# Re-timing the row-halved first layer: attention work ahead at the entry, the reload early in the last tile, three second-layer weights converted during attention

## The chip, the cores and the metric

The kernel runs on one core of one Trainium2 chip. The metric is the device time of one execution in microseconds, the median over repeated runs. Five in-order instruction streams share the work: TensorE (PE, matrix products), VectorE (DVE), ScalarE (ACT), GpSimd (POOL) and SyncE (SP), which issues the DMA transfers. They meet only at semaphores.

## The reference

```
x = attention(q, k, v, i_gate, f_gate, o_gate)   # gated linear attention, 4 x 8 heads, 768 steps, width 40
x = x.transpose(0, 2, 1, 3).reshape(3072, 320)
h = x @ w_in            # first layer, 320 -> 2048
x = relu(h) ** 2 @ w_out   # 2048 -> 320
h = x @ w2_in           # second layer, 320 -> 2048
g = where(h > 0, h, exp(min(h, 0)) - 1)
return g @ w2_out       # 2048 -> 320
```

## The kernel before

Attention is cut into 24 units (u) of chunks; its result, transposed, is the input of the first layer. Both layers work on 6 token tiles j of 512 tokens and on NF = 16 slices m of 128 of the hidden width. A step k stands for one (layer, j, m). Every fp32 operand of a product is held as a high part (rounded for the fast product) and a low part (the difference), so each product is three matmuls.

**First layer.** Tiles j = 0 and 1 use matmuls of all 128 rows (L477 for the first product, L538 for the second). Tiles 2 to 5 use the upper and lower 64 rows of the array as two independent streams ("row halves": L576 first product, L595 second product). They run in `cycle(k, fill)`, one for each four steps (k = 32, 36, ..., 92). A cycle is 62 positions of the two streams; other engines' work is hung on positions by `at(i, f, ...)`, and what stands at a position follows, on its engine, what stands at an earlier one. ACT and DVE apply the relu (L504 on ACT, L502 on DVE), ACT squares (L486), DVE makes the low part `glo` or `gt` (`elem_lo`, L522). `handed` (L561) is a one-element ACT instruction that reads a PSUM bank and so makes the next writer wait for it: its row reads `room`.

The cycles k = 32 to 76 carry attention (`fill_attention`): transposes of the last unit's result (`xt`, L367), value products (L304, L309), `scores` (L292), the DVE multiplication of scores with the mask `mb` (`emit_P`, L299), the normalisation (`norm`, L350 to L353, ending in `xt`), gates (`gate_exp`: `gaw`, L199). Step k = 30 is the entry: it is written out by hand and begins the row-halved form.

**The reload.** The first layer's sums go through `put_bank` (a copy from PSUM: `y`, L602 on ACT, L604 on DVE) to the scratch tensor `y_dr` (L605), and come back for the second layer by `y_load` (`yr`, L827, 768 KB in two DMAs). There is one `yr` buffer. `y_split(j, c)` turns chunk c (of 5) into a high part on ACT (L843) and a low part on DVE (L844).

**Weights.** A weight slice is loaded as packed integers (`raw`, L125), and made into two fp32 parts by `w_top` (`cu`, ACT, L130), `w_low` (`ct`, ACT, L135), `w_add` (DVE, L140), `w_hi` (POOL, L144) and `w_lo` (DVE, L150). The `raw` pool has three buffers; in the cycles with attention two of them are used as `gt`. The 16 slices of the second layer are NF to NF+15. The last tile's cycles (k = 80, 84, 88, 92) carry `fill_last(c)`, c = 0 to 3, which holds the reload of tile 0 and the conversions.

**Second layer.** Pairs of steps: `first_pair(k + 2)` (two first products on the two row halves, L756), then `second_half(k - 2)` and `second_half(k)` (L787). ACT makes `r`, `th`, `ex` (L512 to L514), DVE `ex`, `r` (L515, L516), POOL `ghi` (L517), DVE `glo` (L522). In its tile j = 0 it converts the last slices and splits tile 1's input between the pairs; the later tiles split only.

Of the kernel before, what the change touches and what calls it, by code (L numbers as in the profile page):

```python
# [63 lines left out]
def body(tc, qk, kvo, gates, wq, ident_in, out):  # L64
# [50 lines left out]
    w_n = [0] * 4  # L115

    def w_load(i):
        t = raws[i] = rawp.tile([128, 4 * WC + 32], I16, tag="raw", name="raw")
        l, f = ftiles[i]
        sp.dma_start(out=t[:, 1:1 + 4 * WC], in_=wq[l, f].bitcast(I16))  # L125

    def w_top(i):
        t = tops[i] = cvu.tile([128, WC], F16, tag="cu", name="cu")
        r = raws[i].bitcast(BF16)[:, 4:4 + 4 * WC].rearrange("p (n four) -> p n four", four=4)
        act.activation(out=t, in_=r[:, :, 0], func=AF.Copy)  # L130

    def w_low(i):
        u = low[i] = cvt.tile([128, WC], I32, tag="ct", name="ct")
        r = raws[i].bitcast(U32)[:, 1:1 + 2 * WC].rearrange("p (n two) -> p n two", two=2)
        act.activation(out=u, in_=r[:, :, 0], func=AF.Copy, scale=2.0 ** -13)  # L135

    def w_add(i):
        t = whole[i] = low.pop(i)
        u = t.bitcast(U16).rearrange("p (n two) -> p n two", two=2)[:, :, 1]
        dve.tensor_tensor(out=u, in0=u, in1=tops.pop(i).bitcast(U16), op=ALU.add)  # L140

    def w_hi(i):
        W[ftiles[i]] = wp.tile([128, 2 * WC], F32R, tag="w", name="w")
        pool_.tensor_scalar(out=W[ftiles[i]][:, 0:WC], in0=whole[i].bitcast(F32), scalar1=1.0, scalar2=1.0, op0=ALU.mult, op1=ALU.mult)  # L144

    def w_lo(i):
        l, f = ftiles[i]
        w, t = W[l, f], whole.pop(i)
        for a, k, o in [(640, 64, WC), (0, 640, WC + 64)] if l == 0 else [(0, WC, WC)]:
            dve.tensor_tensor(out=w[:, o:o + k], in0=t[:, a:a + k].bitcast(F32), in1=w[:, a:a + k].bitcast(F32), op=ALU.subtract)  # L150

    def w_next(which, *fs):
        i = w_n[which]
        w_n[which] += 1
        for f in fs:
            f(i)
# [546 lines left out]
    def fill_attention(k):  # L703

        u = (k + 21) // 4
        t = 4 * u + 1
        out = []
        def at(i, f, *a):
            out.append((i, f, *a))
        def products():  # L710
            ps = bank(u, "s")
            if B <= u - 1 < NU:
                for f in trans(u - 1, ps):
                    f()
# [18 lines left out]
        at(36, units, u + 1, scores)  # L733
        at(36, units, u + 1, lambda v: emit_P(2 * v), lambda v: emit_P(2 * v + 1))
        at(38, gate_at, t + 15, gate)
        at(42, gate_at, t + 15, gate_exp)
        at(44, gate_at, t + 15, gate_store)
        at(44, units, u + 1, o_tanh, wk_mult)
        at(45, units, u + 2, lambda v: mask(2 * v), lambda v: mask(2 * v + 1))
        return out  # L740

    def first_pair(k):
# [17 lines left out]
    def second_ops(k, i):  # L760

        l, j, m, _ = steps[k]
        w, cs, ops = W[l, m + 1], slice(i * L, (i + 1) * L), []
        for x in range(2):
            hi, lo, _ = G[k + x]
            wh, wl = (w[:, o + 384 * x:o + 384 * x + DM] for o in (0, WC))
            ops += [(hi[:, cs], wh), (hi[:, cs], wl), (lo[:, cs], wh)]
        return ops

# [60 lines left out]
    def y_split(j, c):  # L830

        t = YR[j]
        if c == 0:
            X[NTILE + j] = []
            for x in range(2):
                if j % 2:
                    a, b_ = (xp.tile([128, n, TT], F32R, tag=tag, name=tag) for n, tag in ((3, "xh"), (3, "xl")))
                    X[NTILE + j].append([a[:, i] for i in range(3)] + [b_[:, i] for i in range(2)])
                else:
                    a = bp["x"].tile([128, 5, TT], F32R, tag=f"x{x}", name=f"x{x}")  # L840
                    X[NTILE + j].append([a[:, i] for i in range(5)])
        hi, lo = (X[NTILE + j][x][c] for x in range(2))
        act.activation(out=hi, in_=t[:, c], func=AF.Copy)  # L843
        dve.tensor_tensor(out=lo, in0=t[:, c], in1=hi.bitcast(F32), op=ALU.subtract)  # L844
        if c == 3:
            dve.tensor_tensor(out=t[:, 4], in0=t[:, 4], in1=t[:, 5], op=ALU.add)

    mp_t = {}
# [122 lines left out]
    }  # L971
    for word in ORDER.split():
        tasks[word[0]](int(word[1:]))
    w_n = [NF] * 4

    nt, nm = NK + 21, NK + 2

    def first(k):
# [6 lines left out]
            nm += 1  # L985
        return todo

    def convert(i):
        w_top(i)
        w_low(i)  # L990
        if i + 3 < 2 * NF:
            w_load(i + 3)
        w_add(i)

    def fill_last(c):

        n = [0, 2, 5, 8, 11][c:c + 2]
        todo = [NF + i for i in range(*n)]
        out = []
        if c == 0:  # L1000
            out += [(0, w_load, NF), (20, w_load, NF + 1), (20, w_load, NF + 2), (20, y_load, 0)]
        if c == 3:
            out += [(0, y_load, 1)]
        if len(todo) > 2:
            i = todo.pop(0)
            out += [(11, convert, i), (12, w_hi, i), (26, w_lo, i)]
        a, b = todo
        out += [(37, convert, a), (45, convert, b), (46, w_hi, a), (57, w_lo, a), (57, w_hi, b), (61, w_lo, b)]
        out += [(i, y_split, 0, x) for i, x in ([(52, 0)], [(18, 1), (52, 2)], [(18, 3), (52, 4)], [])[c]]
        return out  # L1010

    for k in range(NK, len(steps)):
# [15 lines left out]
        if k + 2 == JP * NF:  # L1028
# [7 lines left out]
            attn_mul(t)  # L1036
            for f in mm2(k):
                f()
            zipped(lower, upper)
            elem(k + 2)  # L1040
            elem_lo(k + 2)
            attn_post(t)
            attn_pre(t + 1)
            attn_pe(t + 1)
            for f in mm2(k + 1):
                f()
            elem(k + 3)
            elem_lo(k + 3)
            put(k + 1)
            attn_mul(t + 1)  # L1050
            attn_post(t + 1)
            units((t + 1) // 4, o_tanh, wk_mult)
            units((t + 1) // 4 + 1, lambda v: mask(2 * v), lambda v: mask(2 * v + 1))
# [1 line left out]
            if k % 4 == 0:  # L1055
                cycle(k, fill_last(m // 4) if last else fill_attention(k))
        if l == 0 and k + 2 >= JP * NF:
            w_n = [NF + 14, *[NF + 11] * 3]
            continue
        for t in ts[:-1]:  # L1060
            turn(t)
# [2 lines left out]
        if l:  # L1064
            todo = []
            if k % 2 == 0 and k + 2 < len(steps):
# [13 lines left out]
            todo = first(k + 2)  # L1080
        for t in ts[-1:]:
            attn_pe(t)
        for e in todo:
            elem(e)
        for t in ts[-1:]:
# [2 lines left out]
            elem_lo(e)  # L1088
        for t in ts[-1:]:
            attn_post(t)  # L1090
        if l == 1 and j == 0 and m % 2 == 0 and m:
            if w_n[3] < min(w_n[2], 2 * NF):
                w_next(3, w_hi, w_lo)
            if w_n[1] < min(w_n[0], 2 * NF):
                w_next(1, w_top, w_low)
                w_next(2, w_add)
            if w_n[0] < min(w_n[2] + 3, 2 * NF):
                w_next(0, w_load)
# [26 lines left out]
def _layout(inputs):  # L1125
# [20 lines left out]
    for pre in ("moe_", "moe2_"):  # L1146
# [39 lines left out]
```

## Time and profile before

| | |
|---|---|
| time, median of 3 runs | 827.59 us (825.81 to 829.61) |
| time of the profiled execution | 828.81 us |
| span of the profiled execution | 827.0 us |
| PE busy | 794.5 us, 96% of the span |
| DVE busy | 514.2 us, 62% |
| ACT busy | 494.9 us, 60% |
| POOL busy | 143.1 us, 17% |
| DMA moved | 74.72 MB |

The span is the trace from first to last instruction; the 1.8 us between span and time lie around it. A matmul's busy time is modelled, and at half clock a busy PE does half the work, so the busy share alone does not say how much there is to win: the granted clock of a stretch (PEclk, 1.00 is 2.4 GHz, 0.50 is 1.2 GHz) has to be read beside it.

### The profile page before, as it was taken

Reading aid. Unit: us, or ns where it says so; the run is one execution under the profiler, and the core shown is the slowest. Engines: PE = TensorE matmul, PEld = TensorE weight load, DVE = VectorE, ACT = ScalarE, POOL = GpSimd, SP = SyncE. Lnnn points to the kernel's source line nnn. Section 1 sums busy time; section 2 is a strip of 40 time slices with the busy share of each in tenths; the row PEclk is TensorE's granted clock in tenths of the full one; section 3 lists DMA queues with packets and bytes.
Section 4 is the critical chain, followed back from the end, with each engine's and each line's share of the span. In section 5 each row is a group of like instructions: output and inputs, shape, how many; then the busy total and the mean of one; then the engine's idle time right before and its main releaser. Section 6 shows DMA issues by size and latency. Waiting matters only on the chain.

```text
span 827.0 us, 19680 instructions
## 1 busy us (share of the span) xinstructions
PE 794.5 (96%) x8146; PEld 697.1 (84%) x8146; DVE 514.2 (62%) x882; ACT 494.9 (60%) x1060; POOL 143.1 (17%) x209
## 2 busy tenths in 40 slices
PE   9999999998999999999949989799999999999998
PEld 5688878886988888888948879699999999999997
DVE  6899955454455455343226668777767777677665
ACT  5798756654655665653547867456555555555553
POOL 3234110001000000100001223222222222122121
PEclk9999999998999999999978999899999999999999
DMA  8996332334222323410193732130220300400000
GB/s 234 311 296 217 90 114 79 72 81 145 91 73 71 109 70 92 95 62 2 36 250 110 186 140 72 31 80 2 56 54 2 78 34 2 109 2 2 33 2 33
DMA packets 28554, 74.72 MB, mean 90 GB/s; under 512 B 3376, under 2 KB 6960, under 8 KB 28464
## 3 DMA queue, kind: packets, MB, share of 16 engines
q1 hardware_dynamic: 28176, 73.14, 31.2%
q8 instruction: 64, 1.05, 0.5%
q10 hardware_dynamic: 288, 0.33, 0.1%
q14 instruction: 26, 0.21, 0.1%
HBM read 64.72 MB, written 8.73 MB: 89 GB/s over the span
## 4 chain that ended last, share of the span: by engine, by line
PE 78%; DVE 9%; DMA 5%; ACT 3%; issue 2%; POOL 2%; SPq 0%; POOLq 0%; DVEq 0%; ACTq 0%
PE h L756 18%; PE acc L787 18%; PE h L576 13%; PE acc L595 12%; PE acc L538 4%; PE h L477 4%; PE pv L304 2%; DMA yr<-y_dr 2%; PE in L304 2%; DVE w L150 1%; DMA kvo<-kvo 1%; DMA mb<-negm_dr 1%; PE s L292 1%; DVE ct L140 1%; DVE glo L522 1%
## 5 line engine op out<-in xcount | busy, mean ns | idle before, releaser
L522 DVE TENSOR_TENSOR glo<-r,ghi 128x512 fp32r<-128x512 f32 x168 | 118.4, 708 | 91.8 <-ACT r L486 63.7
L576 PE MATMUL h<-xh,w 64*128 64x512 f32 x640 | 158.0, 401 | 12.1 <-ACT r L504 10.5
L787 PE MATMUL acc<-w,ghi 64*128 64x320 f32 x1472 | 143.1, 306 | 2.9 <-DVE y L604 2.9
L512 ACT ACTIVATE r<-h 128x512 f32<-128x512 f32 x96 | 56.5, 589 | 121.7 <-PE h L756 107.3
L787 PEld LDWEIGHTS acc<-w,ghi 64*128 64x128 f32 x1472 | 123.5, 184 | 5.8 <-issue 3.2
L515 DVE SCALAR_TENSOR_TENSOR ex<-ex,th 128x512 f32<-128x512 f32 x96 | 83.9, 874 | 66.0 <-ACT ex L514 63.3
L517 POOL TENSOR_SCALAR ghi<-r 128x512 fp32r<-128x512 f32 x96 | 74.4, 775 | 263.6 <-DVE r L516 263.6
L576 PEld LDWEIGHTS h<-xh,w 64*128 64x128 f32 x640 | 91.7, 188 | 24.5 <-ACT r L504 10.9
L595 PE MATMUL acc<-ghi,w 64*128 64x512 f32 x400 | 98.7, 392 | 0.0
L756 PE MATMUL h<-x,w 64*128 64x512 f32 x720 | 92.9, 394 | 5.4 <-POOL w L144 5.3
L576 PE MATMUL h<-xl,w 64*128 64x512 f32 x320 | 97.2, 398 | 0.0
L787 PE MATMUL acc<-w,glo 64*128 64x320 f32 x736 | 94.7, 306 | 0.0
L756 PEld LDWEIGHTS h<-x,w 64*128 64x128 f32 x720 | 75.4, 188 | 15.0 <-POOL w L144 5.6
L504 ACT ACTIVATE r<-h 128x512 f32<-128x512 f32 x81 | 47.9, 592 | 62.8 <-PE h L576 47.0
L595 PEld LDWEIGHTS acc<-ghi,w 64*128 64x128 f32 x400 | 67.6, 187 | 4.6
L595 PE MATMUL acc<-glo,w 64*128 64x512 f32 x240 | 70.2, 386 | 0.0
L516 DVE SCALAR_TENSOR_TENSOR r<-h,ex 128x512 f32<-128x512 f32 x96 | 66.4, 691 | 3.3
L787 PEld LDWEIGHTS acc<-w,glo 64*128 64x128 f32 x736 | 66.8, 184 | 0.0
L513 ACT ACTIVATE th<-r 128x512 f32<-128x512 f32 x96 | 60.7, 632 | 3.1
L595 PE MATMUL acc<-gt,w 64*128 64x512 f32 x384 | 61.6, 390 | 0.0
L486 ACT ACTIVATE r<-r 128x512 f32<-128x512 f32 x96 | 59.9, 624 | 1.6
L477 PE MATMUL h<-xh,w 128*128 128x512 f32 x192 | 60.0, 397 | 0.0
(145 smaller groups left out, 1428.0 us busy)
## 6 DMA issues: line engine op xcount, KB each, us to landing
raw<-wq SPq DMA_DIRECT2D x32, 704.0 KB, 6.1
kvo<-kvo SPq DMA_DIRECT2D x24, 488.0 KB, 4.2
mb<-negm_dr SPq DMA_DIRECT2D x40, 256.0 KB, 4.6
rqk<-qk SPq DMA_DIRECT2D x48, 192.0 KB, 5.5
yr<-y_dr SPq DMA_DIRECT2D x12, 768.0 KB, 9.3
y_dr<-y SPq DMA_DIRECT2D x18, 256.0 KB, 4.1
out<-y SPq DMA_DIRECT2D x17, 160.0 KB, 1.8
out<-ct SPq DMA_DIRECT2D x5, 160.0 KB, 1.9
```

Source lines behind the costliest of these rows:

```text
L477: lambda i=i, a=a, b_=b_: pe.matmul(h[:, 0:n], lhsT=a, rhs=b_, start=(i == 0), stop=(i == len(seq) - 1))
L486: act.activation(out=r, in_=r, func=AF.Square)
L512: act.activation(out=r, in_=h, func=AF.Relu, scale=-1.0)
L513: act.activation(out=th, in_=r, func=AF.Tanh, scale=0.5)
L515: dve.scalar_tensor_tensor(out=ex, in0=ex, scalar=1.0, in1=th, op0=ALU.add, op1=ALU.mult)
L516: dve.scalar_tensor_tensor(out=r, in0=h, scalar=0.0, in1=ex, op0=ALU.max, op1=ALU.subtract)
L517: pool_.tensor_scalar(out=hi, in0=r, scalar1=1.0, scalar2=1.0, op0=ALU.mult, op1=ALU.mult)
L522: dve.tensor_tensor(out=lo, in0=r, in1=hi.bitcast(F32), op=ALU.subtract)
L576: pe.matmul(h, lhsT=a, rhs=b_[r, c], start=n == 3 and c + x == 0, stop=c == n - 1 and x == 2, skip_group_check=n == 2)
L595: pe.matmul(ACC[l, j][i], lhsT=a, rhs=b_, start=m == 0 and not again and n == 0, stop=n == len(ops) - 1, skip_group_check=m > 0 or again)
L756: pe.matmul(h[i], lhsT=a[r], rhs=b_[r], start=n == 0, stop=n == len(ops) - 1)
L787: pe.matmul(ACC[l, j][i][:, 0:DM], lhsT=a, rhs=b_, start=m == 0 and not again and n == 0, stop=n == 5 and (not again or m + 2 == NF), skip ...
```

## The change

Seven edits, all to the order of work; nothing is computed differently.

1. Entry (k = 30): `attn_post` (with `norm`) and `attn_pre` come before the second part of the first products and before `elem`; the scores come after that part; `attn_mul` before `mm2(31)`. In the first cycle no attention event stands before position 9.
2. `gate_exp` at position 46 of a cycle instead of 42.
3. Slices NF, NF+1, NF+2 are loaded at position 36 of cycles 64, 68, 72 and converted at position 45 of cycles 68, 72, 76.
4. In the cycle k = 80 `y_load(0)` is the first thing given to SP; three raw loads follow at position 1; chunks 0 and 1 of tile 0 are split at 46 and 52 of that cycle, chunks 2, 3, 4 at 18 of the next three. The conversions in these four cycles are placed anew.
5. Second-layer slices are 640 elements wide instead of 704 (a gap of 64 is dropped).
6. The copy of bank 0 at the start of the second layer moves from DVE (event 10) to ACT (event 6).
7. Tile 0 of the second layer: `w_lo`, `w_add`, `w_hi` stand before the pair's elementwise work instead of behind it; `y_split(1, c)` moves from the pairs m = 2, 4, 6, 8, 10 to m = 0 (c 0), 10 (c 1, 2) and 12 (c 3, 4).

```diff
@@ fill_attention
         def at(i, f, *a):
-            out.append((i, f, *a))
+            out.append((max(i, 9 if begin else 0), f, *a))
...
-        at(42, gate_at, t + 15, gate_exp)
+        at(46, gate_at, t + 15, gate_exp)
...
+        i = NF + (k - (NTILE - 1) * NF) // 4 + 3
+        if i >= NF:
+            at(45, convert, i)
+        if NF - 1 <= i < NF + 2:
+            at(36, w_load, i + 1)
@@ y_split
-        if c == 3:
+        if c == 0:
             dve.tensor_tensor(out=t[:, 4], in0=t[:, 4], in1=t[:, 5], op=ALU.add)
@@ fill_last
-        n = [0, 2, 5, 8, 11][c:c + 2]
-        todo = [NF + i for i in range(*n)]
-        out = []
+        n = NF + 3 * c
+        out = [(18, y_split, 0, c + 1)] if c else [(0, y_load, 0)] + [(1, w_load, n + i) for i in (3, 4, 5)] + [(46, y_split, 0, 0), (52, y_split, 0, 1)]
+        if c:
+            out += [(11, convert, n)] * (c > 1) + [(12, w_hi, n - 1), (26, w_lo, n - 1), (37, convert, n + 1), (45, convert, n + 2)]
+        a, b = n, n + 1
+        out += [(46, w_hi, a), (57 if c < 3 else 50, w_lo, a)]
         if c == 0:
-            out += [(0, w_load, NF), (20, w_load, NF + 1), (20, w_load, NF + 2), (20, y_load, 0)]
...
@@ entry, k + 2 == JP * NF
             for f in mm2(k):
                 f()
+            attn_post(t)
+            attn_pre(t + 1)
             zipped(lower, upper)
+            attn_pe(t + 1)
             elem(k + 2)
             elem_lo(k + 2)
-            attn_post(t)
-            attn_pre(t + 1)
-            attn_pe(t + 1)
+            attn_mul(t + 1)
             for f in mm2(k + 1):
                 f()
             elem(k + 3)
             elem_lo(k + 3)
             put(k + 1)
-            attn_mul(t + 1)
@@ start of the second layer
-                    ends = {6: [lambda: put_bank(NTILE - 1, 1, act)], 10: [lambda: put_bank(NTILE - 1, 0, dve), lambda: put_bank(NTILE - 1, 2, act)]}
+                    ends = {6: [lambda: put_bank(NTILE - 1, 1, act), lambda: put_bank(NTILE - 1, 0, act)], 10: [lambda: put_bank(NTILE - 1, 2, act)]}
@@ its tile 0
+        if l and j == 0 and m % 2 == 0:
+            i = NF + 10 + m // 2
+            if 0 < m < 14:
+                w_lo(i - 1)
+            if 0 < m < 10:
+                w_add(i + 1)
+            if m < 12:
+                w_hi(i)
         for e in todo:
             elem(e)
...
-                    if jn < NTILE and m in (2, 4, 6, 8, 10):
-                        y_split(jn, (m - 2) // 2)
+                    for c in ({0: (0,), 10: (1, 2), 12: (3, 4)} if j == 0 else {2 * c + 2: (c,) for c in range(5)}).get(m, ()) if jn < NTILE else ():
+                        y_split(jn, c)
```

At the entry the change shows on DVE. Before, the instructions from the last state update of a unit to the mask products of the next one (`den` to `xt` is `norm`, `mb` is `emit_P`) stand so:

```order
L342 TENSOR_TENSOR cf_124<-pv,cf_124 40x4x42
L522 TENSOR_TENSOR glo<-r,ghi 128x512
L350 SCALAR_TENSOR_TENSOR den<-num 128x8
L351 RECIPROCAL den<-den 128x8
L352 TENSOR_TENSOR num<-num,den 128x8x40
L353 SCALAR_TENSOR_TENSOR xt<-kvo,num 128x320
L522 TENSOR_TENSOR glo<-r,ghi 128x512
L299 TENSOR_TENSOR mb<-s,mb 128x512
L299 TENSOR_TENSOR mb<-in,mb 128x512
```

With the change the same place reads:

```order
L342 TENSOR_TENSOR cf_124<-pv,cf_124 40x4x42
L350 SCALAR_TENSOR_TENSOR den<-num 128x8
L351 RECIPROCAL den<-den 128x8
L352 TENSOR_TENSOR num<-num,den 128x8x40
L353 SCALAR_TENSOR_TENSOR xt<-kvo,num 128x320
L522 TENSOR_TENSOR glo<-r,ghi 128x512
L299 TENSOR_TENSOR mb<-s,mb 128x512
L299 TENSOR_TENSOR mb<-in,mb 128x512
L522 TENSOR_TENSOR glo<-r,ghi 128x512
```

The first `glo` has moved behind the four instructions of `norm`, and the second behind both mask products.

On SP, from the store of the sums of tile 3 to the second reload, the program before issues:

```order
L605 DMA y_dr<-y 128x512 x3
L125 DMA raw<-wq 128x2816
L605 DMA y_dr<-y 128x512 x3
L125 DMA raw<-wq 128x2816 x2
L827 DMA yr<-y_dr 64x6x512 x2
L125 DMA raw<-wq 128x2816 x8
L827 DMA yr<-y_dr 64x6x512 x2
```

The changed program issues, from the same store:

```order
L605 DMA y_dr<-y 128x512 x3
L128 DMA raw<-wq 128x2560 x3
L833 DMA yr<-y_dr 64x6x512 x2
L128 DMA raw<-wq 128x2560 x3
L605 DMA y_dr<-y 128x512 x3
L128 DMA raw<-wq 128x2560 x6
L833 DMA yr<-y_dr 64x6x512 x2
```

The reload `yr` of tile 0 now stands ahead of the store of tile 4's sums and of three raw loads, and behind three raw loads that belong to attention cycles.

On DVE, the end of tile 0 of the second layer before (from the pair m = 10 to the pair m = 12; `w` is `w_lo`, `ct` is `w_add`, `xl<-yr` is `y_split`):

```order
L522 TENSOR_TENSOR glo<-r,ghi 128x512 x2
L150 TENSOR_TENSOR w<-ct,w 128x704
L140 TENSOR_TENSOR ct<-ct,cu 128x704
L844 TENSOR_TENSOR xl<-yr,xl 128x512
L515 SCALAR_TENSOR_TENSOR ex<-ex,th 128x512
L516 SCALAR_TENSOR_TENSOR r<-h,ex 128x512
L515 SCALAR_TENSOR_TENSOR ex<-ex,th 128x512
L516 SCALAR_TENSOR_TENSOR r<-h,ex 128x512
L522 TENSOR_TENSOR glo<-r,ghi 128x512 x2
L150 TENSOR_TENSOR w<-ct,w 128x704
```

With the change, from the pair m = 10 to the end of the pair m = 12:

```order
L522 TENSOR_TENSOR glo<-r,ghi 128x512 x2
L850 TENSOR_TENSOR xh<-yr,xh 128x512 x2
L156 TENSOR_TENSOR w<-ct,w 128x640
L515 SCALAR_TENSOR_TENSOR ex<-ex,th 128x512
L516 SCALAR_TENSOR_TENSOR r<-h,ex 128x512
L515 SCALAR_TENSOR_TENSOR ex<-ex,th 128x512
L516 SCALAR_TENSOR_TENSOR r<-h,ex 128x512
L522 TENSOR_TENSOR glo<-r,ghi 128x512 x2
L850 TENSOR_TENSOR xl<-yr,xl 128x512 x2
```

The splits stand in twos behind the `glo` of the last two pairs, and `w_lo` ahead of the pair's `ex`.

## Rows read from the trace of the kernel before

**Rows 1.** The page: engine totals, and two DMA kinds (median us to landing last).

```profile
PE 794.5 (96%) x8146; PEld 697.1 (84%) x8146; DVE 514.2 (62%) x882; ACT 494.9 (60%) x1060; POOL 143.1 (17%) x209
...
raw<-wq SPq DMA_DIRECT2D x32, 704.0 KB, 6.1
...
yr<-y_dr SPq DMA_DIRECT2D x12, 768.0 KB, 9.3
```

**Rows 2.** Waits of PE: total us, times, longest us.

```profile
PE h L576 <- ACT r L504: 10.5, 1, 10.5
PE h L756 <- POOL w L144: 5.3, 1, 5.3
PE s L367 <- DVE mb L299: 3.6, 1, 3.6
PE acc L787 <- DVE y L604: 2.9, 1, 2.9
...
PE h L576 <- ACT room L561: 1.2, 2, 0.9
```

**Rows 3.** Timeline at the entry: start us, us, instruction, idle before and its releaser.

```profile
192.07 0.69 DVE L522 TENSOR_TENSOR glo<-r,ghi 128x512 fp32r<-128x512 f32 x1 [6.04 <-ACT r L486]
...
194.50 1.74 POOL L275 TENSOR_SCALAR_AFFINE_SELECT mb<-mb 128x512 f32<-128x512 f32 x2
...
196.61 0.71 PE L367 MATMUL s<-ident,xt 128*128 128x128 f32 x3 [3.60 <-DVE mb L299]
```

**Rows 4.** Windows: length, busy PE PEld DVE ACT POOL, PEclk, DMA share, GB/s.

```profile
197.00:205.00 8.00, 7.90 (x89) 6.58 (x87) 4.78 (x15) 1.71 (x6) 0.00 (x0) 0.59 0.45 161
433.50:440.00 6.50, 6.38 (x31) 4.77 (x33) 3.67 (x6) 3.79 (x8) 0.00 (x0) 0.57 0.10 40
484.00:489.00 5.00, 2.15 (x18) 1.54 (x16) 4.33 (x7) 2.89 (x6) 0.92 (x1) 1.00 0.14 52
...
530.50:536.00 5.50, 5.35 (x28) 3.88 (x30) 2.76 (x4) 0.00 (x0) 0.00 (x0) 0.62 0.19 45
```

**Rows 5.** Timeline at the reload: start of cycle 80 on PE, SP, ACT.

```profile
408.63 0.45 PE L576 MATMUL h<-xh,w 64*128 64x512 f32 x2
...
416.20 1.33 SPq L827 DMA_DIRECT2D yr<-y_dr  x2
...
432.35 0.63 ACT L843 ACTIVATE x<-yr 128x512 fp32r<-128x512 f32 x1 [10.33 <-DMA yr<-y_dr]
```

**Rows 6.** Timeline in attention cycles, ACT and SP: the slack before a relu, the queue.

```profile
348.30 0.35 SPq L231 DMA_DIRECT2D kvo<-kvo  x1
...
376.12 0.60 ACT L504 ACTIVATE r<-h 128x512 f32<-128x512 f32 x1 [2.15 <-PE h L576]
...
418.31 0.81 ACT L135 ACTIVATE ct<-raw 128x704 int32<-128x704 uint32 x1
```

**Rows 7.** Windows of second-layer tile 0 and of tile 1, columns as in Rows 4.

```profile
488.48:552.11 63.63, 58.19 (x628) 54.46 (x630) 49.38 (x66) 36.73 (x70) 16.74 (x21) 0.95 0.22 59
552.11:607.64 55.53, 55.53 (x629) 52.20 (x628) 40.05 (x56) 31.57 (x63) 12.17 (x16) 1.00 0.18 42
```

**Rows 8.** Timeline of DVE in tile 0 of the second layer.

```profile
514.59 1.25 DVE L522 TENSOR_TENSOR glo<-r,ghi 128x512 fp32r<-128x512 f32 x1 [0.52 <-POOL ghi L517]
515.76 0.88 DVE L150 TENSOR_TENSOR w<-ct,w 128x704 fp32r<-128x704 f32 x1
...
523.05 0.88 DVE L150 TENSOR_TENSOR w<-ct,w 128x704 fp32r<-128x704 f32 x1
```

**Rows 9.** Timeline of tile 1, one pair: ACT, PE and DVE.

```profile
571.19 0.60 ACT L512 ACTIVATE r<-h 128x512 f32<-128x512 f32 x1 [2.73 <-PE h L756]
...
576.58 1.54 PE L756 MATMUL h<-xl,w 64*128 64x512 f32 x12
577.61 0.69 DVE L522 TENSOR_TENSOR glo<-r,ghi 128x512 fp32r<-128x512 f32 x1 [0.51 <-POOL ghi L517]
578.22 0.68 DVE L844 TENSOR_TENSOR x<-yr,x 128x512 fp32r<-128x512 f32 x1
```

More of the change, by code (lines that the diff above doesn't have):

```diff
@@ L114, in body, with width @@
     raws, tops, low, whole = {}, {}, {}, {}
-    w_n = [0] * 4
+    def width(i):
+        return WC if i < NF else 2 * DM
     def w_load(i):
+        n = width(i)
         t = raws[i] = rawp.tile([128, 4 * WC + 32], I16, tag="raw", name="raw")
         l, f = ftiles[i]
-        sp.dma_start(out=t[:, 1:1 + 4 * WC], in_=wq[l, f].bitcast(I16))
+        sp.dma_start(out=t[:, 1:1 + 4 * n], in_=wq[l, f, :, 0:n].bitcast(I16))
     def w_top(i):
         t = tops[i] = cvu.tile([128, WC], F16, tag="cu", name="cu")
-        r = raws[i].bitcast(BF16)[:, 4:4 + 4 * WC].rearrange("p (n four) -> p n four", four=4)
-        act.activation(out=t, in_=r[:, :, 0], func=AF.Copy)
+        n = width(i)
+        r = raws[i].bitcast(BF16)[:, 4:4 + 4 * n].rearrange("p (n four) -> p n four", four=4)
+        act.activation(out=t[:, 0:n], in_=r[:, :, 0], func=AF.Copy)
     def w_low(i):
         u = low[i] = cvt.tile([128, WC], I32, tag="ct", name="ct")
-        r = raws[i].bitcast(U32)[:, 1:1 + 2 * WC].rearrange("p (n two) -> p n two", two=2)
-        act.activation(out=u, in_=r[:, :, 0], func=AF.Copy, scale=2.0 ** -13)
+        n = width(i)
+        r = raws[i].bitcast(U32)[:, 1:1 + 2 * n].rearrange("p (n two) -> p n two", two=2)
+        act.activation(out=u[:, 0:n], in_=r[:, :, 0], func=AF.Copy, scale=2.0 ** -13)
     def w_add(i):
         t = whole[i] = low.pop(i)
-        u = t.bitcast(U16).rearrange("p (n two) -> p n two", two=2)[:, :, 1]
-        dve.tensor_tensor(out=u, in0=u, in1=tops.pop(i).bitcast(U16), op=ALU.add)
+        n = width(i)
+        u = t.bitcast(U16).rearrange("p (n two) -> p n two", two=2)[:, 0:n, 1]
+        dve.tensor_tensor(out=u, in0=u, in1=tops.pop(i).bitcast(U16)[:, 0:n], op=ALU.add)
     def w_hi(i):
         W[ftiles[i]] = wp.tile([128, 2 * WC], F32R, tag="w", name="w")
-        pool_.tensor_scalar(out=W[ftiles[i]][:, 0:WC], in0=whole[i].bitcast(F32), scalar1=1.0, scalar2=1.0, op0=ALU.mult, op1=ALU.mult)
+        pool_.tensor_scalar(out=W[ftiles[i]][:, 0:width(i)], in0=whole[i][:, 0:width(i)].bitcast(F32), scalar1=1.0, scalar2=1.0, op0=ALU.mult, op1=ALU.mult)
     def w_lo(i):
@@ L148, in w_lo @@
         w, t = W[l, f], whole.pop(i)
-        for a, k, o in [(640, 64, WC), (0, 640, WC + 64)] if l == 0 else [(0, WC, WC)]:
+        for a, k, o in [(640, 64, WC), (0, 640, WC + 64)] if l == 0 else [(0, 2 * DM, WC)]:
             dve.tensor_tensor(out=w[:, o:o + k], in0=t[:, a:a + k].bitcast(F32), in1=w[:, a:a + k].bitcast(F32), op=ALU.subtract)
[L152 to L156, printed above, removed]
     m_st = gc.tile([64, NCH + 1], F32, name="m_st")
@@ L707, in fill_attention @@
         out = []
+        begin = k == JP * NF
         def at(i, f, *a):
-            out.append((i, f, *a))
+            out.append((max(i, 9 if begin else 0), f, *a))
         def products():
@@ L765, in second_ops @@
             hi, lo, _ = G[k + x]
-            wh, wl = (w[:, o + 384 * x:o + 384 * x + DM] for o in (0, WC))
+            wh, wl = (w[:, o + DM * x:o + DM * x + DM] for o in (0, WC))
             ops += [(hi[:, cs], wh), (hi[:, cs], wl), (lo[:, cs], wh)]
@@ L973, in body @@
         tasks[word[0]](int(word[1:]))
-    w_n = [NF] * 4
     nt, nm = NK + 21, NK + 2
@@ L986, in first, with stage, convert @@
         return todo
-    def convert(i):
+    def stage(i):
         w_top(i)
         w_low(i)
-        if i + 3 < 2 * NF:
+        if NF + 2 < i and i + 3 < 2 * NF:
             w_load(i + 3)
+    def convert(i):
+        stage(i)
         w_add(i)
     def fill_last(c):
-        n = [0, 2, 5, 8, 11][c:c + 2]
-        todo = [NF + i for i in range(*n)]
-        out = []
+        n = NF + 3 * c
[4 more added lines that the diff above has]
+        out += [(46, w_hi, a), (57 if c < 3 else 50, w_lo, a)]
         if c == 0:
-            out += [(0, w_load, NF), (20, w_load, NF + 1), (20, w_load, NF + 2), (20, y_load, 0)]
-        if c == 3:
+            out += [(57, convert, n + 3)]
+        if c < 3:
+            out += [(57, w_hi, b), (61, w_lo, b)]
+        else:
             out += [(0, y_load, 1)]
[L1004 to L1009, printed above, removed]
         return out
@@ L1057, in body @@
         if l == 0 and k + 2 >= JP * NF:
-            w_n = [NF + 14, *[NF + 11] * 3]
             continue
@@ L1090, in body @@
             attn_post(t)
[L1091 to L1098, printed above, removed]
+        if l and j == 0 and m in (0, 2, 4, 6):
+            stage(NF + 12 + m // 2)
         jn = j + 1 if l else 0
@@ L1156, in _layout @@
             for x in range(2):
-                w[:, 1, :, 384 * x:384 * x + DM] = wo[x::2]
+                w[:, 1, :, DM * x:DM * x + DM] = wo[x::2]
             ws.append(w.reshape(NF, 128, WC))
```

## The prediction, made before the changed kernel ran

> **What bounds the kernel now.** I read the page first. PE is busy for 794.5 of 827.0 us [rows 1], so only what leaves PE idle or at half clock can be won back; the other four streams matter where PE waits for them. Next I read the waits of PE, which say where the idle time is. From the start of the row-halved layer on there are five places: 10.5 us for an ACT relu, 5.3 for a POOL weight, 3.6 for a DVE mask, 2.9 for a DVE copy, and 1.2 in two waits for a bank mark [rows 2]. The third view is the windows, for the clock: after the 3.6 us wait the granted clock averages 0.59 over 8.0 us, after the 10.5 us wait 0.57 over 6.5 us, after the 5.3 us wait 0.62 over 5.5 us, while around the 2.9 us wait it stays at 1.00 [rows 4]. A long idle of PE is therefore paid twice. Last I read the timeline at each place, for what was late.
>
> At the entry the mask of the next unit is late. POOL makes it only at 194.50, behind `xt`, and `xt` stands on DVE behind a `glo` that began at 192.07 after 6.04 us of waiting for ACT; PE goes on at 196.61 [rows 3]. At the reload, SP issues `yr` at 416.20, behind stores and weight loads, and ACT gets the data only at 432.35 [rows 5]: 16 us, where the median of such a reload is 9.3 [rows 1]. The relu that PE needs stands on ACT behind that split. In tile 0 of the second layer DVE sets the pace: the same weight operation begins at 515.76 and 523.05 [rows 8], 7.29 us per pair of steps, while tile 1 takes 55.53 us for its 8 pairs, 6.94 each [rows 7]. The lag grows until a weight is late for PE.
>
> **The change part by part.**
>
> Entry. With the four `norm` instructions ahead of the `glo`, `xt` no longer waits for ACT, and POOL can make the mask during the 6 us in which DVE was idle. The mask product then waits only for the scores. The 3.6 us go, and the half clock with them: 8.0 x (1 - 0.59) = 3.3. The smaller of the two bank waits (1.2 - 0.9 = 0.3) lies in the same place. Together 7.2. The moved `glo` is now needed by the second product of the first cycle, which comes after that cycle's first products, so it has cover. If the products are late in their new place, at most the old 3.6 us return, with their clock.
>
> `gate_exp`. The 0.9 us wait is for a bank mark behind a `gaw` on ACT; at position 46 `gaw` comes after the mark. Gain 0.9.
>
> Attention cycles 64 to 76. SP has issued its last attention load at 348.30 [rows 6], so the three new loads hold up nobody. Each is converted about one cycle later. A cycle without attention is 14.4 us long: the one that starts at 408.63 ended where PE stopped, 10.5 us before 433.5 [rows 2, 4, 5]; one with attention is longer. A raw load takes 6.1 us [rows 1]. ACT gets two conversions of 0.81 x 640/704 = 0.74 us in each of three cycles, 1.5 us. They stand where ACT waits for PE, 2.15 us long before the relu at 376.12 [rows 6]. So I cost them at nothing; if the cover failed, 1.5 us in each of three cycles, 4.5, would show.
>
> Reload. `yr` is first in the queue of cycle 80, and nothing but three weight loads of the cycles before stands ahead of it, so it can go when its buffer is free, at or before 408.63 where that cycle starts [rows 5]. ACT came to the first split at 432.35 - 10.33 = 422.0, then at position 52; at 46 it comes to it at about 420, an estimate. With the observed 16 us the reload is in time if issued by 404, with the median by 411. The weight loads that follow it are converted at position 57 or later. Gain 10.5 + 6.5 x (1 - 0.57) = 13.3 [rows 2, 4].
>
> Bank copy. DVE's copy stood behind a pair's elementwise work; on ACT it comes with the other two copies, earlier. ACT is busy 2.89 of 5.0 us there [rows 4], so it has room. Gain 2.9; the clock was at full speed anyhow. If ACT were late by one copy, half a microsecond would remain.
>
> Tile 0 of the second layer. Per pair DVE loses a split of 0.68 [rows 9] and 64 of 704 elements in two weight operations (0.08 each, from the 0.88 of one [rows 8]): 7.29 - 0.84 = 6.45, under 6.94. PE should set the pace again, and 63.63 - 55.53 = 8.1 us come back [rows 7]. The splits come back as a new wait, though. Chunks 3 and 4 are split in the pair m = 12, behind its `glo`. In the regular pair of tile 1 ACT's relu begins at 571.19 and a split that follows the last `glo` (577.61) runs from 578.22 to 578.90, 7.7 us after the relu; the last two chunks of the next first pair begin at 576.58, 5.4 us after, and need the first low part one matmul pair later, at 5.6 [rows 9]. So PE waits 2.1 us at m = 14. The fifth chunk's split (0.68) ends about when its own matmuls come. Between 0, if DVE runs ahead of the regular pair, and 2.8, if it lags by another split, I take 2.1. At the first pairs of this tile the order is new and DVE is behind by what it converts first; I put 0.4 there, an estimate between 0 and one 0.88 us operation.
>
> One rule of the Trainium skill bears on this DVE sum. First the row: a `glo` that overlaps POOL's weight part takes 1.25 us [rows 8], the one of tile 1 takes 0.69 [rows 9], so an overlap costs 0.56, and it is in the 7.29 already. The Trainium skill, SBUF — State Buffer, section "Who interferes with whom", says that a DVE instruction with two SBUF inputs and a GpSimd instruction that reads SBUF exclude one another for a whole instruction. By that rule the POOL part, now ahead of the pair's work, could block a second DVE instruction; with another 0.56 the pair would be 7.0, just over 6.94, and the tile would lose some 0.5 us more.
>
> The sum: 7.2 + 0.9 + 13.3 + 2.9 + 8.1 = 32.4, less 2.1 and 0.4, is 29.9. From the profiled execution's 828.8 us that gives 798.9. The median of the shown runs is 1.2 lower, which would give 797.7; I forecast **798.5**.
>
> **The rivals.**
>
> A. DVE stays behind in tile 0, or the new wait costs clock too. For it: the split pairs and the POOL parts crowd the same engine. The half clock would add 5.5 x (1 - 0.62) = 2.1 us [rows 4], a repeated late `glo` about 2. Against it: 6.45 per pair, and the 2.9 us wait that left the clock at 1.00. Time 801 to 803. The Trainium skill speaks for it: TensorE: Matmul & The Clock Gate, section "A second HAM failure mode: psum-queue depth-cycling", says that PE idling often in small pieces can oscillate between the two clocks; no stretch here shows that after an idle under 3 us.
>
> B. The entry wait only moves: the scores or the delayed products keep 3.6 us, with clock 6.9. Time 802 to 806. Against it: the mask's makers are idle there.
>
> C. The conversions lengthen three attention cycles by 1.5 us each. Time 803.
>
> D. The reload is not earlier, because its buffer or a weight load in front of it holds SP. The 13.3 us stay: 812. Against it: a queue that is empty after 348.30.
>
> E. Slower. In cycles 68, 72 and 76 the conversion stands on ACT ahead of the relu that PE waits for, just as the split did at the reload. If each raw load came too late by the 10 us of that case, each cycle would lose 13.3 us; three make 39.9, and the time would be 838. It decides (slower than 828 by more than noise) from three such cycles on (two give 825). It would need a load that lands about 14.4 + 10 = 24 us after its issue, against the median of 6.1 [rows 1]; that it could not be issued until a `gt` buffer is free is what speaks for it.
>
> F. No new wait at m = 14: 796.5.
>
> **How the numbers follow.** The main case has 0.60 and its own range of 797 to 801. A has 0.15, B 0.10, C 0.05, D 0.04, E 0.015, F 0.045. From 796 to 806 the main case, A, B, C and F are held, about 0.9; leaving out F's lower half and B's end it is still above 0.8, and I give **796 to 806**. A change under 0.5% (4.1 us) can hardly be told from none in this kernel. Faster by more than that: all but E and some unforeseen loss of the same size, 0.965; within it 0.015 (two of E's cycles); slower 0.02.
>
> **What would show it.** In the changed profile: no PE wait for a mask at the entry, and a clock near 1.00 there; no ACT wait for the reload, which is issued before cycle 80 starts, and a cycle 80 and 84 of 14.4 us each; no DVE copy ahead of the second half; tile 0 of the second layer about 58 us, with one PE wait of about 2 us for a split near its end, at full clock. Attention cycles longer than before would show C; a clock of 0.5 after the wait at m = 14 would show A. The prediction would be wrong if a `raw` or `gt` buffer comes free later than I read, or if the first cycle, with its attention events all at position 9 or later, runs out of its own cover.

## The result and the profile after

The changed kernel takes 796.76 us (median of 4 runs, 795.54 to 797.09) against 827.83 us for the kernel before (4 runs): a ratio of 0.9623, 95% interval 0.9598 to 0.9647. The profiled execution went from 828.81 to 797.03 us, 31.8 us less. The forecast was 798.5 us in a range of 796 to 806, so the time lies near the lower end of the range.

The page first, the engine totals and the granted clock of the 40 slices (tenths of full speed):

```profile
PE 785.0 (99%) x8142; PEld 685.9 (86%) x8146; DVE 510.7 (64%) x881; ACT 493.7 (62%) x1061; POOL 144.0 (18%) x209
...
PEclk9999999999999999999999999999999999999999
```

PE is busy for 99% of the span instead of 96% [rows 1], and every slice of the clock shows 9 (0.9 or more). The waits of PE (total us, times, longest us):

```profile
PE in L367 <- DVE xt L353: 1.8, 1, 1.8
PE h L762 <- DVE xl L850: 1.4, 1, 1.4
PE dps L907 <- POOL dr L903: 1.3, 1, 1.3
PE in L367 <- DVE mb L299: 0.9, 1, 0.9
...
PE h L576 <- DVE r L502: 0.2, 1, 0.2
```

All five waits of [rows 2] are gone. From the row-halved layer on, the new one for a split (`xl`, L850), 1.4 us, is left, with 0.2 us for a DVE relu and 0.2 us for a `glo` at the very end. The others lie before the entry. The windows of the same places as [rows 4] and of tile 0 (length, busy PE PEld DVE ACT POOL, PEclk, DMA share, GB/s):

```profile
194.00:202.00 8.00, 8.00 (x116) 6.88 (x114) 5.25 (x16) 6.61 (x19) 0.45 (x2) 1.00 0.65 181
406.00:440.00 34.00, 33.80 (x297) 31.59 (x295) 22.03 (x28) 26.22 (x55) 6.21 (x7) 1.00 0.43 138
462.00:508.00 46.00, 46.00 (x516) 43.21 (x514) 41.09 (x56) 32.68 (x63) 15.92 (x21) 1.00 0.10 37
508.00:512.00 4.00, 2.63 (x26) 1.93 (x24) 2.17 (x4) 0.40 (x1) 0.75 (x1) 1.00 0.01 4
```

The entry, the reload and tile 0 up to m = 12 have a PE that is full but for 0.2 us at the reload, at a clock of 1.00; the last window, 4 us long, holds 1.37 us of idle time. The reload on SP and its first split on ACT, against [rows 5]:

```profile
342.33 41.00 SPq L128 DMA_DIRECT2D raw<-wq  x3
383.43 1.34 SPq L833 DMA_DIRECT2D yr<-y_dr  x2
...
410.62 1.15 ACT L849 ACTIVATE x<-yr 128x512 fp32r<-128x512 f32 x2
```

`yr` is issued at 383.43 instead of 416.20, right behind the third of the three raw loads (issued at 342.33, 366.79 and 383.00). No reload of this run took more than 11.5 us to land, so it lies ready long before ACT comes to it at 410.62; that row shows no wait.

To see where the 31.8 us arose I took the start of the same instruction in both traces. The last column is what was won since the line above.

| instruction | before | after | won |
|---|---|---|---|
| last wide second product before the entry (L538) | 187.63 | 187.27 | 0.4 |
| value products of the cycle k = 36 (L309) | 219.03 | 211.70 | 7.0 |
| the same, k = 56 | 309.38 | 300.85 | 1.2 |
| first ACT relu of the cycle k = 80 (L504) | 413.78 | 405.31 | -0.1 |
| last ACT relu of k = 84 | 449.42 | 427.89 | 13.1 |
| last of k = 92 | 471.65 | 449.24 | 0.9 |
| ACT relu of tile 0, m = 2 (L512) | 493.94 | 468.07 | 3.5 |
| the same, m = 12 | 536.47 | 502.77 | 7.8 |
| the same, m = 14 | 543.41 | 511.60 | -1.9 |
| first relu of tile 1 | 552.13 | 520.33 | 0.0 |

### The profile page after: what moved, and what is told of

Its sections match the earlier page's. It is cut to its first block, busy times and chain, and to the rows that moved or that the text cites. A ratio compares the mean times of both kernels' runs of the same rounds, so it can differ in the third digit from the quotient of the medians.

```text
span 795.2 us, 19678 instructions
## 1 busy us (share of the span) xinstructions
PE 785.0 (99%) x8142; PEld 685.9 (86%) x8146; DVE 510.7 (64%) x881; ACT 493.7 (62%) x1061; POOL 144.0 (18%) x209
## 4 chain that ended last, share of the span: by engine, by line
PE 86%; DVE 6%; DMA 3%; issue 2%; POOL 1%; ACT 1%; SPq 1%; DVEq 0%; POOLq 0%; ACTq 0%
PE h L762 21%; PE acc L793 20%; PE acc L595 14%; PE h L576 14%; PE acc L538 5%; PE h L477 4%; PE pv L304 2%; DMA kvo<-kvo 2%; PE s L292 2%; PE in L304 2%; DMA mb<-negm_dr 1%; DVE w L156 1%; POOL w L150 1%; DVE ct L146 1%; PE s L367 1%
## 5 line engine op out<-in xcount | busy, mean ns | idle before, releaser
L576 PE MATMUL h<-xh,w 64*128 64x512 f32 x640 | 152.6, 393 | 0.2 <-DVE r L502 0.2
L793 PE MATMUL acc<-w,ghi 64*128 64x320 f32 x1472 | 146.0, 306 | 0.0
L512 ACT ACTIVATE r<-h 128x512 f32<-128x512 f32 x96 | 56.6, 589 | 114.4 <-PE h L762 97.6
L515 DVE SCALAR_TENSOR_TENSOR ex<-ex,th 128x512 f32<-128x512 f32 x96 | 81.6, 850 | 63.8 <-ACT ex L514 60.7
L576 PEld LDWEIGHTS h<-xh,w 64*128 64x128 f32 x640 | 88.1, 184 | 10.4 <-DVE r L502 0.6
L793 PE MATMUL acc<-w,glo 64*128 64x320 f32 x736 | 96.9, 306 | 0.0
L576 PE MATMUL h<-xl,w 64*128 64x512 f32 x320 | 93.0, 391 | 0.0
L504 ACT ACTIVATE r<-h 128x512 f32<-128x512 f32 x81 | 47.9, 592 | 60.6 <-PE h L576 44.8
L762 PEld LDWEIGHTS h<-x,w 64*128 64x128 f32 x720 | 72.7, 184 | 10.6
```

Source lines behind the costliest of these rows:

```text
L512: act.activation(out=r, in_=h, func=AF.Relu, scale=-1.0)
L515: dve.scalar_tensor_tensor(out=ex, in0=ex, scalar=1.0, in1=th, op0=ALU.add, op1=ALU.mult)
L576: pe.matmul(h, lhsT=a, rhs=b_[r, c], start=n == 3 and c + x == 0, stop=c == n - 1 and x == 2, skip_group_check=n == 2)
L762: pe.matmul(h[i], lhsT=a[r], rhs=b_[r], start=n == 0, stop=n == len(ops) - 1)
L793: pe.matmul(ACC[l, j][i][:, 0:DM], lhsT=a, rhs=b_, start=m == 0 and not again and n == 0, stop=n == 5 and (not again or m + 2 == NF), skip ...
```

## The experiments

Eight kernels ran, in two groups; the kernel before ran along with each group (medians 828.57 and 828.60 us).

**Which part of edit 4 wins the reload?** The first experiment is the kernel before with only the reload moved:

```diff
-            out += [(0, w_load, NF), (20, w_load, NF + 1), (20, w_load, NF + 2), (20, y_load, 0)]
+            out += [(0, y_load, 0), (0, w_load, NF), (20, w_load, NF + 1), (20, w_load, NF + 2)]
```

> The kernel before with one edit: the reload of tile 0 is the first thing SP gets in the cycle k = 80, ahead of the first raw load, instead of last at position 20. Theory (the reload was late because of its place in SP's queue): the 10.5 us wait of PE and its half clock go, -13 us, about 814.5 us; a wait of up to 1.5 us for a raw load may be left. Rival (three weights out of the way in the attention cycles are what made the room): the wait moves to a raw load behind the reload, less than half of it is won, 820 us or more.

Measured: 816.91 us (814.91 to 817.82), ratio 0.984 (0.9799 to 0.9882), 11.7 below the kernel before. Its SP queue and the ACT rows around the split:

```profile
381.20 2.04 SPq L827 DMA_DIRECT2D yr<-y_dr  x2
397.56 0.36 SPq L125 DMA_DIRECT2D raw<-wq  x1
411.39 3.27 SPq L605 DMA_DIRECT2D y_dr<-y  x3
...
419.23 0.84 ACT L130 ACTIVATE cu<-raw 128x704 f16<-128x704 bf16 x1 [1.56 <-DMA raw<-wq]
...
420.69 0.62 ACT L843 ACTIVATE x<-yr 128x512 fp32r<-128x512 f32 x1
```

ACT no longer waits for `yr`. What is left is the 1.56 us wait for a raw load that the first reading allowed for, and PE waits of 0.8 us for a DVE relu and 0.4 for an ACT relu. Between the same relus as in the table, from the first of k = 80 to the last of k = 84, this kernel takes 23.57 us, against 35.64 before and 22.58 in the changed kernel: 12.1 of the 13.1 us. Cycles 88 and 92 take 22.25 us, against 22.23 and 21.35: none of the 0.9.

Why the place counts for so much stands in SP's own waits in the kernel before:

```profile
SPq L125 <- DVE gt L522: 38.6, 1, 38.6
```

This is the first raw load of the cycle k = 80. From the end of the stores of tile 3, at 350.8, SP stood in front of it until 399.07, most of the time for a `gt` buffer to come free; the stores of tile 4 followed at 412.90, when their data were made. The reload stood behind both. It was late because of what its predecessors in the queue waited for, and also because 16 us passed from its issue to its use [rows 5], where the median to landing is 9.3 [rows 1].

The opposite edit, in the changed kernel, moves the reload back behind the raw loads and the stores:

```diff
-        ... [(0, y_load, 0)] + [(1, w_load, n + i) for i in (3, 4, 5)] + ...
+        ... [(1, w_load, n + i) for i in (3, 4, 5)] + [(20, y_load, 0)] + ...
```

> The changed kernel with the reload of tile 0 moved back to position 20 of the cycle k = 80, behind the three raw loads and the stores of tile 4; the three weights stay in the attention cycles. Theory (the place in SP's queue is what counts): issued at about 408, landed after some 13 us beside those transfers, while ACT comes to the split at 410.6; a PE wait of about 8 us and half clock behind it, +10 us against the changed kernel, about 807. Rival (with three weights out of the way the reload is quick, the median 9.3 us): +5 us or less, 802 or below.

Measured: 808.91 us (806.97 to 811.88), ratio 0.9766 (0.9727 to 0.9805), 12.2 above the changed kernel. The stage from the first relu of k = 80 to the last of k = 84 takes 33.35 us, 10.8 more than in the changed kernel. The timeline of SP and ACT:

```profile
409.43 2.61 SPq L605 DMA_DIRECT2D y_dr<-y  x3
412.10 1.99 SPq L833 DMA_DIRECT2D yr<-y_dr  x2
...
424.92 1.15 ACT L849 ACTIVATE x<-yr 128x512 fp32r<-128x512 f32 x2 [10.25 <-DMA yr<-y_dr]
```

and the first of its waits of PE:

```profile
PE h L576 <- ACT r L504: 8.1, 1, 8.1
```

The transfer takes 12.8 us from issue to use, PE waits 8.1 us, and the clock behind it averages 0.64 from 426 to 434. So the place in the queue wins this stage; the three weights that went into the attention cycles were not needed for it. The rest of the two stages, 1.0 and 0.9 us, came with the other re-timings of the last tile, the three weights among them; what each of these is worth was not measured by itself.

**Is the entry worth a stall and a clock?** The kernel before with edit 1 alone (the entry's reordering and the `max(i, 9 if begin else 0)`, both as in the diff above).

> The kernel before with the entry's new order alone (and attention events at position 9 or later in the first cycle). Theory (stall plus half clock): -7.0 us, about 820.8 us, and a granted clock of 1.00 from 194 to 205. Rival (only the idle is won, the clock falls for another reason): -3.6 us, about 824.2.

Measured: 821.87 us (820.18 to 824.45), ratio 0.9897 (0.9847 to 0.9946), 6.7 below the kernel before. PE doesn't wait for the mask at the entry any more, and the windows answer the clock:

```profile
194.00:202.00 8.00, 8.00 (x116) 6.79 (x114) 5.61 (x16) 6.62 (x19) 0.05 (x1) 1.00 0.51 171
197.00:205.00 8.00, 8.00 (x119) 7.45 (x115) 6.21 (x16) 5.96 (x17) 1.46 (x3) 1.00 0.64 194
```

The stretch that ran at 0.59 [rows 4] runs at 1.00 with the idle gone. The interval, 4.5 us or more won, leaves out the 3.6 us of the rival. The first theory holds.

**The two small edits.** In the changed kernel `gate_exp` stands at 42 again, and bank 0 is copied by DVE at event 10:

```diff
-        at(46, gate_at, t + 15, gate_exp)
+        at(42, gate_at, t + 15, gate_exp)
...
-                    ends = {6: [lambda: put_bank(NTILE - 1, 1, act), lambda: put_bank(NTILE - 1, 0, act)], 10: [lambda: put_bank(NTILE - 1, 2, act)]}
+                    ends = {6: [lambda: put_bank(NTILE - 1, 1, act)], 10: [lambda: put_bank(NTILE - 1, 0, dve), lambda: put_bank(NTILE - 1, 2, act)]}
```

> The changed kernel with two small edits undone, which lie 200 us apart and are read apart in the trace: gate_exp at position 42, and the copy of bank 0 on DVE at event 10. Theory: PE waits 0.9 us for the bank mark behind gaw (about 1.2 us longer in the cycle) and about 2.9 us for the copy, with the clock at 1.00 around both: +4.1 us, about 801. Rival: the copy was only late because DVE was overloaded by the conversions around it, which now stand elsewhere: under 1 us for it, 798.

Measured: 799.51 us (799.13 to 800.29), ratio 0.9648 (0.9607 to 0.9689), 2.75 above the changed kernel. The two rows in its waits of PE:

```profile
PE acc L793 <- DVE y L604: 1.2, 1, 1.2
...
PE h L576 <- ACT room L561: 0.9, 1, 0.9
```

The 0.9 us came back as expected. The copy costs 1.2 us, not 2.9: this falls between the readings. In the kernel before, two weight parts stood on DVE between the two `ex` of that pair, the later one behind a wait for POOL:

```profile
483.71 0.89 DVE L150 TENSOR_TENSOR w<-ct,w 128x704 fp32r<-128x704 f32 x1 [1.26 <-POOL w L144]
```

Here the last weight part is done by 458.0, before the pair's first `ex` at 459.40. So less than half of the 2.9 us belongs to the copy's move. By these rows the rest came from the conversions' new places in the last tile; that part was not tested by itself.

**The new wait at m = 14.** Two other placements of tile 1's splits, in the changed kernel:

```diff
-                    for c in ({0: (0,), 10: (1, 2), 12: (3, 4)} if j == 0 else ...
+                    for c in ({0: (0,), 8: (1,), 10: (2, 3, 4)} if j == 0 else ...
```

> The changed kernel with the splits of tile 1 at m = 0 (chunk 0), 8 (1) and 10 (2, 3, 4), none at m = 12. Theory (the wait at m = 14 is the low part of chunks 3 and 4 made a pair too late): no PE wait for a split, -1.4 to -1.9 us against the changed kernel, about 795.1. Rival (three splits in one pair make that pair's successor late by as much): a wait for glo in its place, 796.5 to 798.

```diff
-                    for c in ({0: (0,), 10: (1, 2), 12: (3, 4)} if j == 0 else {2 * c + 2: (c,) for c in range(5)}).get(m, ()) ...
+                    for c in ({2 * c + 2: (c,) for c in range(5)}).get(m, ()) ...
```

> The changed kernel with the splits of tile 1 at their old pairs, m = 2, 4, 6, 8, 10, one each. Theory (narrower weights and the new order leave slack): DVE takes 6.48 + 0.68 = 7.16 us per pair against 6.94, the lag of 0.8 us at m = 4 grows to about 1.6 by m = 10, under the 2.5 us of cover, so PE doesn't wait: about 795.1. Rival (DVE is the bound again, as in the kernel before): a PE wait of 3 us or more comes back, perhaps with half clock, 798 to 802.

Measured: 794.48 us (793.51 to 796.52), ratio 0.9574 (0.9541 to 0.9607), and 794.20 us (793.02 to 796.69), ratio 0.9573 (0.9539 to 0.9606). In both the wait for a split is gone and nothing takes its place; the window that held it is full, here that of the second kernel:

```profile
500.00:511.00 11.00, 11.00 (x133) 10.86 (x131) 7.83 (x12) 6.87 (x13) 2.68 (x3) 1.00 0.67 139
```

They are 2.3 and 2.6 us below the changed kernel by the medians, somewhat more than the 1.9 us that its m = 14 lost in the table. Their intervals overlap with its own, so the times alone don't show the difference. The traces do: from the first relu of the pair m = 0 to the first relu of tile 1 the two take 56.31 and 56.30 us, the changed kernel 58.21. The second is the changed kernel with the splits of tile 1 left where they were before: this part of edit 7 cost 1.9 us, and without it nothing waits. They are the fastest versions here. In the second, DVE's `w_lo` follow each other by 7.09 us (482.32, 489.41, 496.49), more than PE's 6.94, and PE doesn't wait.

**Why did tile 0 run late before?** The last two kernels start from that second placement. One makes the weights 704 wide again, which undoes edit 5 (it makes each conversion shorter, so it is less work and not only another order):

```diff
-        return WC if i < NF else 2 * DM
+        return WC
...
-        for a, k, o in [(640, 64, WC), (0, 640, WC + 64)] if l == 0 else [(0, 2 * DM, WC)]:
+        for a, k, o in [(640, 64, WC), (0, 640, WC + 64)] if l == 0 else [(0, WC, WC)]:
```

> The kernel with the splits of tile 1 at m = 2, 4, 6, 8, 10 (e4), and second-layer weights 704 wide again. Theory (DVE per pair 6.48 + 0.68 + 0.16 = 7.32 against 6.94 lets the lag grow by 0.38 per pair, to 2.3 us, just under its cover of about 2.5): 0 to 1 us of PE wait, 794.2 to 796. Rival (any pace above 6.94 brings the old wait back): a wait of 3 us or more with half clock, 799 or above.

Measured: 795.49 us (795.06 to 796.58), ratio 0.9602 (0.9574 to 0.9631). DVE now repeats after 7.29 us (`w_lo` at 476.89, 484.18, 491.47), the very pace of the kernel before [rows 8], and the only row of tile 0 among the waits of PE is this:

```profile
PE h L762 <- DVE w L156: 0.2, 1, 0.2
```

Its median is 1.3 us above the kernel it starts from, and the intervals overlap; between the same two relus of tile 0 it takes 57.19 us against 56.30, 0.9 more. The old wait of 5.3 us is not there.

What else differs from the kernel before in this tile is when a slice is made. Edit 7 moves the parts within a pair, and the change also spreads them over more pairs, which its list does not say. The old wait is for slice NF+14, which was finished only in the pair right ahead of the first products that need it, those of m = 12. Before, it got `w_top`, `w_low` and `w_add` in the pair m = 8, and `w_hi` and `w_lo` in m = 10 behind the elementwise work:

```profile
529.71 0.78 POOL L144 TENSOR_SCALAR w<-ct 128x704 fp32r<-128x704 f32 x1
```

In the changed kernel it gets `w_top` and `w_low` in m = 4, `w_add` in 6, `w_hi` in 8 and `w_lo` in 10, these three ahead of the elementwise work.

The last kernel puts `w_lo`, `w_add` and `w_hi` behind the pair's elementwise work again, but leaves them in their new pairs, so it is not the old order in full:

```diff
-        if l and j == 0 and m % 2 == 0:
-            i = NF + 10 + m // 2
-            ...
         for e in todo:
             elem(e)
...
         for t in ts[-1:]:
             attn_post(t)
+        if l and j == 0 and m % 2 == 0:
+            i = NF + 10 + m // 2
+            ...
```

> The kernel e4 with w_lo, w_add and w_hi of tile 0 behind the pair's elementwise work, as in the kernel before. Theory (a weight made behind the glo of one pair is needed at the start of the next, about 4 us earlier): a PE wait of about 4 us for a weight at m = 12 and half clock behind it, 800. Rival (the pace of DVE alone made the old wait, and 7.16 us per pair is slow enough for the order not to matter): no PE wait, 794.2.

Measured: 810.66 us (808.88 to 814.69), ratio 0.9789 (0.9755 to 0.9823), 16.5 above the kernel it starts from. Its first two waits of PE:

```profile
PE acc L793 <- ACT room L798: 5.7, 3, 2.5
PE h L762 <- DVE w L156: 4.4, 1, 4.4
```

The 4.4 us wait is the one that the first theory had, for the low part of NF+14 at m = 12. In the timeline of DVE and PE:

```profile
510.40 0.69 DVE L515 SCALAR_TENSOR_TENSOR ex<-ex,th 128x512 f32<-128x512 f32 x1 [0.53 <-ACT ex L514]
...
516.10 0.81 DVE L156 TENSOR_TENSOR w<-ct,w 128x640 fp32r<-128x640 f32 x1
...
516.97 5.33 PE L762 MATMUL h<-x,w 64*128 64x512 f32 x26 [4.44 <-DVE w L156]
```

DVE was not behind in this pair: it waited 0.53 us for ACT before the first `ex`. The place of `w_lo` behind the pair is enough for the wait.

The larger part, 5.7 us, neither theory had. The timeline of ACT from one pair to the next:

```profile
498.91 0.78 ACT L140 ACTIVATE ct<-raw 128x640 int32<-128x640 uint32 x1 [4.29 <-DVE w L156]
499.60 0.14 ACT L798 ACTIVATE room<-acc 1x1 f32<-1x1 f32 x1
499.65 0.61 ACT L849 ACTIVATE xh<-yr 128x512 fp32r<-128x512 f32 x1
500.17 0.57 ACT L512 ACTIVATE r<-h 128x512 f32<-128x512 f32 x1
```

`w_low` on ACT writes a `ct` buffer, of which there are three, that the late `w_lo` still reads. So ACT stands for 4.3 us in three pairs, and with it the bank mark, the split and the next relu behind it, for which PE waits. The pairs there take 9.66 us (`w_lo` at 488.34 and 498.00). The kernel before has no such wait of ACT, so these 5.7 us come from the mixture of the two orders and say nothing about the old one.

## Why the prediction was right, point by point

**Entry, 7.2 us forecast, 7.0 won.** Stall and half clock both went, as the entry alone shows. Rival B, that the wait only moves, didn't happen.

**`gate_exp`, 0.9 forecast, 1.2 won.** Undoing it brings back a 0.9 us wait. The remaining 0.3 of the stage was not traced.

**Attention cycles, 0 forecast, 0.1 lost.** The conversions fit into ACT's slack (rival C falls). For E's mechanism there is no sign: no conversion in these cycles waits for a raw load. The sentence that the three loads hold up nobody was not quite right: two of them wait in the queue until 366.79 and 383.00, and the reload goes only behind the third, 21.9 us before the first relu of the cycle k = 80, against 31.1 us in the first experiment, where no raw load stood ahead of it. This costs nothing, since it is still 27 us before ACT needs it.

**Reload, 13.3 forecast, 13.1 won,** and rival D's loss didn't come. The step was right in its cause too: the reload's place alone, in the kernel before, wins 12.1 of it. The prediction named the stores and weight loads ahead of the reload and its slow landing; that SP stood 48 us in front of the first of those loads it didn't say.

**Cycles 88 and 92, nothing forecast, 0.9 won.** This term was missing. In the kernel before DVE's relu at the end of cycle 84 began only at 450.35, behind a `w_add` and a split, 0.9 us after ACT's relu at 449.42; after the change the two begin at 427.98 and 427.89. The next cycle ends with the same lag: 464.89 against 463.92 before, 442.03 against 441.95 after. That this lag is what the 0.9 us are was not tested.

**Bank copy, 2.9 forecast, 3.5 won in its stage,** but the step gave the whole to the copy. Undoing it costs 1.2 us; the rest was, by the rows, DVE's work ahead of it, which the re-timed conversions took away. That the size came out near is in part luck.

**Tile 0, 8.1 forecast, 7.8 won up to m = 12.** DVE's pace was forecast at 6.45 us per pair and is 6.49 (`w_lo` at 477.31, 483.79, 490.29). The pair of 7.0, in which a second DVE instruction would have been blocked, did not come. But the step named the pace as the cause, and the record says otherwise. In the kernel before, PE kept its 6.94 us per pair up to m = 10 (relus at 500.88, 507.82, 514.76, 521.70), and the loss came in one piece at m = 12, with the wait for NF+14. At 7.29 us per pair, with the weights made earlier and ahead of the pair, PE waits 0.2 us; with the weights behind the pair it waits 4.4 us for the same slice although DVE is not behind. So it was the order that removed the old wait, the place in the pair and the earlier pairs together; how much each of these two gives was not separated. A pace above 6.94 only lets a lag grow, and in this tile the last slice that PE needs early comes at m = 12, just when the lag of the 7.29 us kernel has used up its cover. That 8.1 was nearly right rests on the difference of two measured tiles, which holds whatever the cause.

**The new wait, 2.1 and 0.4 forecast, 1.9 and none lost.** The mechanism is the one described, at m = 14 and on chunk 3's low part, but the wait itself is 1.37 us; the other 0.5 go with it when the splits are moved, but no row shows where they lie. The timeline of the changed kernel at m = 12 and 14 (ACT, DVE, PE):

```profile
502.77 0.60 ACT L512 ACTIVATE r<-h 128x512 f32<-128x512 f32 x1 [2.00 <-PE h L762]
...
506.26 0.69 DVE L515 SCALAR_TENSOR_TENSOR ex<-ex,th 128x512 f32<-128x512 f32 x1
...
508.78 0.69 DVE L522 TENSOR_TENSOR glo<-r,ghi 128x512 fp32r<-128x512 f32 x1 [0.51 <-POOL ghi L517]
...
509.39 1.28 DVE L850 TENSOR_TENSOR xl<-yr,xl 128x512 fp32r<-128x512 f32 x2
...
510.13 1.43 PE L762 MATMUL h<-xl,w 64*128 64x512 f32 x10 [1.37 <-DVE xl L850]
```

The first split begins 6.6 us after the relu, not the 7.0 of the regular pair [rows 9], since the second `ex` is 0.69 us long here; and PE stops at 508.76, 6.0 us after the relu, where 5.6 was forecast. The size was off by 0.7, the place was right. The clock stayed at 1.00 through it, so rival A's price was not paid. The forecast of 798.9 for the profiled execution missed 797.03 by 1.9: 0.6 at the new wait and the early pairs, 0.9 in cycles 88 and 92, 0.4 ahead of the entry; the differences of the other steps cancel. F's 796.5 is nearer to the measured 796.76 us than the 798.5 of the forecast, but by luck: the wait that F left out was there.

## What to carry to other kernels

A transfer that is needed at a known time goes into the queue ahead of transfers that are needed later, above all ahead of those that wait for a buffer or for data: here it was issued more than 20 us earlier for it, and the place in the queue was worth 12 us and the other work around it under 2. Where an engine is a little slower than the one it feeds, look at the order before the load: what the next stage needs first has to stand first, and what frees a buffer for a third engine counts as needed first too. Add the half clock to a long stall, in the cost of a stall and in the worth of removing it: behind the five stalls of 3.6 to 10.5 us shown here the granted clock averaged 0.57 to 0.71 over 5.5 to 8 us.

## What the runs showed of the hardware that was not expected

The prediction took the 2.9 us wait of the kernel before, with the clock at 1.00 around it [rows 4], as a sign that a new wait of 2.1 us would not cost clock. The window from the end of that wait on shows the same:

```profile
488.00:492.00 4.00, 3.52 (x40) 3.47 (x42) 3.56 (x6) 2.22 (x5) 0.62 (x1) 1.00 0.36 133
```

That doesn't hold in general. In the kernel with the weights behind, PE waited 2.29 us before 480.48, 2.46 us before 499.80 and 4.44 us before 516.97, and the windows show:

```profile
482.00:486.00 4.00, 4.00 (x44) 3.96 (x44) 3.31 (x5) 2.92 (x6) 0.62 (x1) 0.76 0.00 0
...
494.00:498.00 4.00, 3.34 (x30) 2.42 (x26) 3.45 (x4) 0.62 (x1) 2.10 (x3) 1.00 0.01 4
498.00:502.00 4.00, 2.20 (x24) 2.21 (x26) 2.35 (x5) 3.06 (x7) 0.00 (x0) 0.87 0.00 0
502.00:506.00 4.00, 4.00 (x38) 3.83 (x36) 3.68 (x5) 2.25 (x5) 1.00 (x2) 0.70 0.00 0
...
518.00:524.00 6.00, 6.00 (x50) 5.08 (x48) 0.00 (x0) 1.64 (x3) 0.00 (x0) 0.71 0.86 181
```

After 2.29 and 2.46 us of idle the clock was at its lower level for part of the time behind; after 1.37 us in the changed kernel it was not. So rival A's case, an idle under 3 us that costs clock, for which the prediction had no row, does have rows here. A wait of about 2.5 us can thus cost more than its length, and what decides between these cases and the 2.9 us one stays open.
